# An agent attention with a gated feed-forward on one core: the planner's rule for column tiled TensorE steps, and the due times of the agents' stage

## The chip, the cores and the metric

The kernel runs on one core of one Trainium2 chip. The metric is the device time of one execution in microseconds (us), read as the median of several runs.

## The reference

For four batches of 12608 tokens of 128 values the reference computes attention through 49 agents, and puts each token through a feed-forward of width 1024. All in float32:

```python
s = 1 / sqrt(128)
agent_v = softmax(s * agents @ k.T) @ v          # per batch, 49 x 128
x = softmax(s * q @ agents.T) @ agent_v          # 12608 x 128
h = x @ w_in                                     # 1024 wide
u = h * softmax(h)
ln = (u - mean(u)) / sqrt(var(u) + 1e-6) * g_ln
out = ln @ w_out
```

The three weight arrays are in double precision and are converted on the chip.

## The kernel before, in words

**Agents' stage** (`phase_a`, one per batch). The 12608 keys of a batch go in 13 chunks of 1024 (the last has 320). M1 (`p1_mm`, L418) multiplies the agents with a chunk's keys. The two halves of a chunk land on the two halves of the 128 partitions, so that each matmul fills 64 of TensorE's 128 columns: a **column tiled** step. Then come a maximum (L423), an exponential (L444), a transpose on TensorE (TT, L451), a copy (L457) and M2 (`p2_mm`, L467), which multiplies with the values, again in two halves of 64 columns, and is added up on VectorE (L476). After chunk 13 a short chain ends the softmax and multiplies the result with `w_in`, which gives the batch's 49 x 1024 matrix, split into a high and a low part. This stage of batch 0 is the head of the kernel. That of batch b + 1 is fed in between the tiles of batch b.

**Queries' stage** (`phase_b`, one per unit). A unit is 8 tiles of 128 queries; a batch has 13 units. B0 (`b0`, L647) multiplies a unit's queries with the agents. It is column tiled too, two matmuls of 64 columns a tile. A maximum (L653), a subtraction (L659), an exponential, a sum and a reciprocal follow, then GpSimd's packing into high and low parts (B4, L676 to L680) and a transpose (B5, L687).

**Tiles** (99 a batch, 396 in all). For tile x, H (`c_h`, L730) gives 1024 columns in one of two wide PSUM tiles; VectorE takes the row maximum (MX, L734), ScalarE the exponential (L744), VectorE the product (U, L749) and ScalarE the sum of squares (SQ, L755). T (`c_t`, L762) transposes u in two halves, ScalarE copies the halves out (L777, L781), and VectorE or GpSimd makes high and low parts (L786, L790, L794). W (`c_w`, L810) is the last product, 24 matmuls for two tiles, into an accumulator's bank that a group of four tiles shares. GpSimd works out the scaling, which goes through DRAM to all partitions, and VectorE applies it (FIN, L875), which frees the bank.

**PSUM.** The two wide tiles aside, four banks serve everything: M1, M2, TT, B0, B5, T, the accumulators of W and a few small products. Each takes a bank and holds it until VectorE or ScalarE has read it.

**What sets the order.** The class `Plan` (L26) simulates the five queues when the kernel is built, and the order in which it places the steps is the order of the instructions on each engine; the last loop of the kernel pins it. Each step has an engine, a planned cost, a due time in units of tiles, the steps it depends on, and on TensorE a kind: 0 for H and W, 1 for transposes and others, 2 for the column tiled M1, M2 and B0. In `run`, for each engine, the steps that can start within `EPS` (0.01 us for TensorE) of the earliest one are the choice, and the one with the lowest due time goes first:

```python
s, o = min((z for z in opts if z[0] <= low + self.EPS[e]), key=lambda z: z[1].due)
```

A step that takes a bank can start no earlier than a bank is free in the simulation. `SWITCH[a][b]` is added to the planned cost of a step of kind b that follows kind a.

Due times of a tile's steps are x plus a constant (DH for H, DMX for the maximum, DT for T, DSQ for the squares, DF_ for FIN, and so on); DHR, DMXR and the like are added in the first 12 tiles, those ending in L in the last batch. B0 of the unit that starts with tile `first` is due at `first - BD0`, its later steps at `first` minus BD1 to BD5. In the agents' stage time runs in planned us: chunk c starts at z = 2.55 c, out of 38.15 in all (`total`, L552), and `at` (L553) spreads these over the batch: from ASTART before its first tile to AEND after its end, 99 + 2.04 + 3.67 = 104.71 tiles. M1 of a chunk (L574) is due at `at(z)`, M2 (L584) at `at(z + 1.5)`. M1 of chunk c waits for TT of chunk c - 2; M2 waits for its copy, the values and M2 of chunk c - 1. K and V chunks are loaded by SyncE, each two chunks ahead at most, since their buffers are two.

Of the kernel before, what the change touches and what calls it, by code (L numbers as in the profile page):

```python
# [25 lines left out]
class Plan:  # L26
# [3 lines left out]
           "AA": 0.0, "AG": 0.17, "GP": 0.25, "GD": 0.1, "GG": 0.1, "GA": 0.2}  # L30
    EPS = {"P": 0.01, "A": 0, "D": 0.07, "G": 2.6, "S": 0.0}

    SWITCH = ((0.0, 0.0, 0.0), (0.0, 0.0, 0.0), (0.087, 0.033, 0.033))

    def __init__(self, banks):
        self.banks = [[0.0, b] for b in banks]
# [25 lines left out]
    def run(self, idle=None):  # L62
        while True:
            best = None
            for e, ops in self.cand.items():
                if not ops:
                    continue
                free = [b[0] for b in self.banks if b[0] is not None]
                first = min(free) if free else None
                at, opts, low = self.at[e], [], None  # L70
                for o in ops:
                    s = max(at, o.ready[e])
                    if o.take:
                        if first is None:
                            continue
                        s = max(s, first)
                    opts.append((s, o))
                    low = s if low is None else min(low, s)
                if low is None:
                    continue  # L80
                s, o = min((z for z in opts if z[0] <= low + self.EPS[e]), key=lambda z: z[1].due)
                if o.shy > 0.0:
                    s, o = min((z for z in opts if z[0] <= s + o.shy), key=lambda z: z[1].due)
                if best is None or s < best[0]:
                    best = (s, e, o)
            if best is None:
                break
            s, e, o = best
# [17 lines left out]
            else:  # L106
                c = o.cost[o.eng.index(e)] if len(o.eng) > 1 else o.cost
# [18 lines left out]
def kernel(  # L126
# [15 lines left out]
    P = 128  # L142
# [4 lines left out]
    NCK = N // (CT * P)  # L147
# [7 lines left out]
    UB = 8  # L155
# [1 line left out]
    WC = 4  # L157

    BD0 = 13.69
    BD1 = 15.3  # L160
    BD2 = 9.96
    BD3 = -17.37
    BD4 = 0.17
    BD5 = 5.85
    DH = -3.24
    DMX = -8.66
    DEX = 0.61
    DU_ = -1.62
    DSQ = 20.92
    DT = -0.42  # L170
    DEV = -8.39
    DLD = 1.53
    DSP = -1.16
    DW = 3.3
    DR = 1.58
    DF_ = 5.14
    OUTD = -5.86
    OUTC = -74.58
    VA = 7
# [5 lines left out]
    SHY = -2.99  # L185
    DHR = -4.68
    DHL = -5.42
    DMXR = 10.02
    DMXL = 15.46
    DEXR = 5.1  # L190
    DEXL = -1.93
    DUR = -10.64
    DUL = -12.84
    DSQR = -10.36
    DSQL = -12.17
    DTR = -6.53
    DTL = -23.81
    DEVR = -0.65
    DEVL = 9.51
    DLDR = -16.59  # L200
    DLDL = 26.96
    DSPR = -6.09
    DSPL = 14.43
    DWR = 2.46
    DWL = -0.21
    RBL = 6.0
    ASTART = -3.67
    AEND = -2.04
    engs = (mybir.EngineType.PE, mybir.EngineType.Activation, mybir.EngineType.DVE, mybir.EngineType.Pool)
    SCALE = 1.0 / math.sqrt(C)  # L210
    INV = 1.0 / DF
# [151 lines left out]
    op = plan.op  # L363
# [9 lines left out]
    def phase_a(b, due, gate):  # L373

        head = b == 0
# [170 lines left out]
        def st(f, *x):  # L546
            return lambda *y: f(*x, *y)
# [2 lines left out]
        sz = lambda c: 0.524 if c < NCK else 0.164  # L550
        fr = lambda c: 1.0 if c < NCK else 0.5
        total = NC * 2.55 + 5.0  # L552
        at = lambda z: due[0] + (due[1] - due[0]) * z / total  # L553
        bg = op("G", begin, 0.0, at(0), gate)
        K, M1, E1, N1, V, M2, EE, TT, ET, AC = ({} for _ in range(10))

# [12 lines left out]
        for c in range(NC):  # L569
            kop(c)  # L570
            if not head:
                kop(c + 1)
            z = c * 2.55
            M1[c] = op("P", st(p1_mm, c), (0.876 if c < NCK else 0.449) + (0.8 if head and c == 0 else 0.0), at(z),  # L574
                       [K[c], M1.get(c - 1), TT.get(c - 2)], take=True, kind=2)
            E1[c] = op("D", st(p1_max, c), 0.6, at(z + 0.3), [M1[c], bg])
            N1[c] = op("D", st(p1_nm, c), 0.07, at(z + 0.4), [E1[c], N1.get(c - 1)])
            EE[c] = op("A", st(p1_exp, c), 0.665 if c < NCK else 0.742, at(z + 0.5), [N1[c], TT.get(c - 2)], free=M1[c])
            if c:
                FC[c] = op("A", st(p1_fc, c), 0.2, at(z + 0.6), [N1[c], AC.get(c - 4)])  # L580
            TT[c] = op("P", st(p2_t, c), 0.435 * fr(c), at(z + 1), [EE[c], M2.get(c - 2)], take=True)
            ET[c] = op(ETE, st(p2_et, c), (0.478 * fr(c), 0.6 * fr(c)), at(z + 1.2), [TT[c]], free=TT[c])
            vop(c)
            M2[c] = op("P", st(p2_mm, c), 1.043 if c < NCK else 0.485, at(z + 1.5),  # L584
                       [ET[c], V[c], M2.get(c - 1), AC.get(c - 2)], take=True, kind=2)
            AC[c] = op("D", st(p2_ev, c), 0.26, at(z + 1.8), [M2[c], FC.get(c), AC.get(c - 1)], free=M2[c])
        if head:
# [2 lines left out]
        z = NC * 2.55 - 1.5  # L590
# [10 lines left out]
        z = NC * 2.55 + 1.0  # L601
# [32 lines left out]
    def phase_b(k, dues, gate=()):  # L634
# [61 lines left out]
        prev, first = None, None  # L696
        for j0, j1 in chunks:
            f = (lambda px, j0=j0, j1=j1: b0(j0, j1, px)) if prev is None else (lambda j0=j0, j1=j1: b0(j0, j1))
            o = op("P", f, 0.155 * (j1 - j0), dues[0] + 0.1 * j0,
                   [BQ[k], prev, B0.get(k - 1)] + [B4.get((k - 2, q)) for q in range(2)] + list(gate), take=prev is None, kind=2, shy=shy)  # L700
            first = first or o
            prev = o
# [222 lines left out]
    def at(x, d, r, l):  # L925
        return x + d + (r * (1.0 - x / 12.0) if x < 12 else l if x >= (B - 1) * TB else 0.0)
# [4 lines left out]
    for x in range(n):  # L931
# [54 lines left out]
        if j == GT - 1:  # L986
            first, rest, turn, sent, d0, d1, d2 = c_rstd(G)
            o = None
# [72 lines left out]
```

## Time and profile before

| what | value |
|---|---|
| median of 3 runs | 1573.73 us (1573.48 to 1576.07) |
| the profiled execution | 1575.81 us, its span 1574.0 us |
| busy: TensorE, ScalarE, VectorE, GpSimd | 1550.8, 1440.1, 1376.5, 1254.5 us |
| granted TensorE clock, mean | 0.999 of full speed |
| moved by DMA | 133.65 MB |

The span runs from the first to the last instruction. Busy time of TensorE counts matmuls; they are pipelined and their ends are modelled, so that rows overlap, and the distance between two starts says more than a duration. Weight loads are rows of their own (PEld). In a timeline, equal instructions that follow each other are one row, with their count at the end. A float32 matmul shows as two records, so M1 of a full chunk is 4 records, M2 is 16 and B0 of a full unit is 32.

### The profile page before, as it was taken

The page shows a single profiled execution, that of the slowest core. Times are in us where ns is not written, and L with a number is a line of the kernel's source. Part 1 is how long each engine was busy: PE and PEld are TensorE (multiplying, and loading weights), DVE is VectorE, ACT ScalarE, POOL GpSimd, SP SyncE. Part 2 cuts the span into 40 slices and gives each one's busy share as a digit, 9 for nine tenths or more (in the row PEclk, how much of TensorE's full clock was granted, in tenths as well). Part 3 has the DMA queues.
Part 4 walks back from the last instruction along what each step waited for, and adds up shares of the span by engine and source line. Part 5 has one row for each costly group of instructions (what it writes and reads, how often), then busy time and mean ns, then how long its engine had stood idle before and what let it go on. Part 6 is the DMA issues. An engine that isn't in the chain of part 4 may idle for free.

```text
span 1574.0 us, 35069 instructions
## 1 busy us (share of the span) xinstructions
PE 1550.8 (99%) x12821; PEld 1381.7 (88%) x12821; DVE 1376.5 (87%) x2161; ACT 1440.1 (91%) x2740; POOL 1254.5 (80%) x1715
## 2 busy tenths in 40 slices
PE   8899999999999999999999999999999999999998
PEld 5588898998889899898899899898988989999998
DVE  6989898888998888889898888988888998989986
ACT  3599999999999999999999998999989999999996
POOL 2577888888788788787888878887878889988896
PEclk9999999999999999999999999999999999999999
DMA  9422323313123223222222232222111121111111
GB/s 370 150 88 81 96 81 95 95 59 103 62 82 100 82 88 105 91 81 74 88 68 88 88 102 88 88 88 87 49 63 53 47 69 55 62 55 49 45 42 40
DMA packets 57629, 133.65 MB, mean 85 GB/s; under 512 B 9840, under 2 KB 14064, under 8 KB 57456
## 3 DMA queue, kind: packets, MB, share of 16 engines
q1 hardware_dynamic: 57456, 131.41, 26.2%
q8 instruction: 101, 1.65, 0.4%
q14 instruction: 72, 0.59, 0.1%
HBM read 105.36 MB, written 26.02 MB: 83 GB/s over the span
## 4 chain that ended last, share of the span: by engine, by line
PE 89%; DVE 4%; ACT 3%; POOL 2%; issue 1%; DMA 0%; SPq 0%; DVEq 0%; ACTq 0%; POOLq 0%
PE px L810 33%; PE ph L730 22%; PE px L762 21%; PE px L647 3%; PE px L467 3%; PE px L418 3%; PE px L687 3%; PE px L451 1%; ACT e L744 1%; DVE u L749 1%; ACT sq L755 1%; DVE nm L734 1%; POOL uL L794 0%; ACT uT L781 0%; DVE mxp L423 0%
## 5 line engine op out<-in xcount | busy, mean ns | idle before, releaser
L794 POOL TENSOR_TENSOR uL<-uT,uH 128x1024 fp32r<-128x1024 f32 (+1 forms) x295 | 598.6, 2029 | 24.3
L734 DVE TENSOR_REDUCE nm<-ph 128x1 f32<-128x1024 f32 x396 | 480.3, 1219 | 55.3 <-PE ph L730 53.3
L749 DVE SCALAR_TENSOR_TENSOR u<-ph,e 128x1024 f32<-128x1024 f32 x396 | 481.0, 1219 | 54.2 <-ACT e L744 30.3
L755 ACT ACTIVATE sq<-u,su 128x1024 bf16<-128x1024 f32 x396 | 464.0, 1172 | 25.9 <-DVE u L749 22.8
L744 ACT ACTIVATE e<-ph,nm 128x1024 f32<-128x1024 f32 x396 | 446.3, 1132 | 28.4 <-DVE nm L734 25.0
L810 PE MATMUL px<-uL,wH 128*128 128x256 f32 x1584 | 467.2, 295 | 0.1
L810 PE MATMUL px<-uH,wH 128*128 128x256 f32 x1584 | 453.5, 286 | 2.6 <-DVE uL L786 1.4
L810 PE MATMUL px<-uH,wL 128*128 128x256 f32 x1584 | 449.4, 284 | 0.0
L762 PE MATMUL px<-ident,u 128*128 128x128 f32 x3168 | 429.4, 274 | 2.6 <-DVE u L749 0.7
L762 PEld LDWEIGHTS px<-ident,u 128*128 128x128 f32 x3168 | 355.6, 141 | 51.5 <-issue 18.7
L790 POOL TENSOR_SCALAR uH<-uT 128x1024 fp32r<-128x1024 f32 (+1 forms) x295 | 268.3, 909 | 85.7 <-ACT uT L781 84.6
L730 PE MATMUL ph<-mh,pT 128*128 128x512 f32 x792 | 326.3, 412 | 0.7 <-DVE u L749 0.4
L810 PEld LDWEIGHTS px<-uH,wH 128*128 128x128 f32 x1584 | 299.7, 189 | 15.4 <-issue 3.8
L730 PE MATMUL ph<-ml,pT 128*128 128x512 f32 x792 | 312.4, 394 | 0.0
L810 PEld LDWEIGHTS px<-uH,wL 128*128 128x128 f32 x1584 | 300.2, 189 | 9.6
L810 PEld LDWEIGHTS px<-uL,wH 128*128 128x128 f32 x1584 | 299.8, 189 | 9.0 <-issue 4.6
L781 ACT COPY uT<-px 128x512 f32<-128x512 f32 x492 | 272.9, 594 | 13.7 <-issue 3.0
L786 DVE TENSOR_TENSOR uL<-px,uH 128x512 fp32r<-128x512 f32 x300 | 200.9, 681 | 28.0 <-ACT uH L777 27.7
L777 ACT CAST uH<-px 128x512 fp32r<-128x512 f32 x300 | 170.1, 603 | 2.9 <-PE px L762 2.6
L730 PEld LDWEIGHTS ph<-mh,pT 128*128 128x128 f32 x792 | 149.2, 188 | 22.6 <-DVE u L749 4.6
L730 PEld LDWEIGHTS ph<-ml,pT 128*128 128x128 f32 x792 | 149.7, 189 | 17.1 <-DVE ml L543 0.2
L829 POOL TENSOR_TENSOR y<-x,nhalf 128x4 f32<-128x4 f32 x99 | 100.1, 1011 | 7.5
(119 smaller groups left out, 1469.2 us busy)
## 6 DMA issues: line engine op xcount, KB each, us to landing
rB<-dr SPq DMA_DIRECT2D x98, 256.0 KB
qt<-in_qT_dram SPq DMA_DIRECT2D x48, 512.0 KB
out_dram<-ob SPq DMA_DIRECT2D x95, 256.0 KB
kt<-in_kT_dram SPq DMA_DIRECT2D x36, 512.0 KB
vt<-in_v_dram SPq DMA_DIRECT2D x36, 512.0 KB
dr<-yr SPq DMA_DIRECT2D x392, 0.5 KB
kh<-in_kT_dram SPq DMA_DIRECT2D x12, 512.0 KB
vh<-in_v_dram SPq DMA_DIRECT2D x12, 512.0 KB
```

The lines of the kernel that those rows point to most:

```text
L730: nc.tensor.matmul(ph[:, sl], lhs, bmats[b]["mh" if m == 0 else "ml"][:, sl], start=(m == 0), stop=(m == 1))
L734: nc.vector.tensor_reduce(out=nms[x], in_=phs[x], op=ALU.max, axis=AX.X, negate=True)
L744: nc.scalar.activation(out=es[x], in_=phs[x], func=AF.Exp, bias=nms.pop(x), accum_out=st[G]["S"][:, j : j + 1])
L749: nc.vector.scalar_tensor_tensor(out=u, in0=phs[x], scalar=INV, in1=es[x], op0=ALU.mult, op1=ALU.mult, accum_out=su)
L755: nc.scalar.activation(out=sq, in_=u, func=AF.Square, bias=su, scale=-float(DF), accum_out=st[G]["Q"][:, j : j + 1])
L762: nc.tensor.transpose(pt[:, kf * P : (kf + 1) * P], us[x][0][:, k0 * P : (k0 + 1) * P], ident)
L777: nc.scalar.copy(out=uH, in_=pt)
L781: nc.scalar.copy(out=rr[x][:, hf * 4 : hf * 4 + 4, :], in_=pt)
L786: nc.vector.tensor_tensor(out=uL, in0=pt, in1=uH.bitcast(F32), op=ALU.subtract)
L790: nc.gpsimd.tensor_scalar(out=uH, in0=rr[x][:, k0:k1, :], scalar1=1.0, scalar2=0.0, op0=ALU.mult, op1=ALU.add)
L794: nc.gpsimd.tensor_tensor(out=uL, in0=rr[x][:, k0:k1, :], in1=uH.bitcast(F32), op=ALU.subtract)
L810: nc.tensor.matmul(po, wt[:, kf, :], ut[:, kf, :], start=(q == 0), stop=(q == WM - 1))
```

## The change

The planner gets a new constant, HOLD. If TensorE's last step was column tiled (`self.kind == 2`), the choice is first narrowed to column tiled steps that can start within 0.3 us of the earliest step of any kind; only if there is none does it go as before. Planned costs of entering and leaving the column tiling are changed, and those of M1, M2 and B0. The agents' stage of batches 1 to 3 is no longer spread over the batch but set to a pace: M1 of a chunk is due every 8 x 0.85 tiles, and M2 at z + 5.38 instead of z + 1.5. Many constants of due times are changed. No instruction is added or removed.

```diff
-    SWITCH = ((0.0, 0.0, 0.0), (0.0, 0.0, 0.0), (0.087, 0.033, 0.033))
+    SWITCH = ((0.0, 0.0, 0.12), (0.0, 0.0, 0.12), (0.18, 0.14, 0.0))
+
+    HOLD = 0.3
...
-                s, o = min((z for z in opts if z[0] <= low + self.EPS[e]), key=lambda z: z[1].due)
+                near = [z for z in opts if z[0] <= low + self.EPS[e]]
+                if e == "P" and self.kind == 2:
+                    near = [z for z in opts if z[0] <= low + self.HOLD and z[1].kind == 2] or near
+                s, o = min(near, key=lambda z: z[1].due)
...
-    BD1 = 15.3
-    BD2 = 9.96
-    BD3 = -17.37
-    BD4 = 0.17
+    BD1 = 13.69
+    BD2 = 4.55
+    BD3 = -15.03
+    BD4 = -7.65
-    DH = -3.24
-    DMX = -8.66
+    DH = -3.44
+    DMX = 1.93
-    DU_ = -1.62
-    DSQ = 20.92
-    DT = -0.42
+    DU_ = -2.24
+    DSQ = 25.67
+    DT = 0.29
-    DLD = 1.53
+    DLD = 0.4
-    DW = 3.3
-    DR = 1.58
-    DF_ = 5.14
+    DW = 3.29
+    DR = 2.85
+    DF_ = 10.2
-    DMXR = 10.02
+    DMXR = 7.04
-    DUR = -10.64
+    DUR = -14.51
-    DSQL = -12.17
-    DTR = -6.53
+    DSQL = -12.71
+    DTR = -16.28
-    DLDL = 26.96
+    DLDL = 27.03
-    ASTART = -3.67
-    AEND = -2.04
+    ASP = 0.85
+    MZ = 5.38
+    ASTART = -6.32
+    AEND = -4.19
...
-        at = lambda z: due[0] + (due[1] - due[0]) * z / total
+        at = lambda z: due[0] + (due[1] - due[0]) * z / total if head else due[0] + UB * ASP * z / 2.55
...
-            M1[c] = op("P", st(p1_mm, c), (0.876 if c < NCK else 0.449) + (0.8 if head and c == 0 else 0.0), at(z),
+            M1[c] = op("P", st(p1_mm, c), (0.95 if c < NCK else 0.51) + (0.8 if head and c == 0 else 0.0), at(z),
...
-            M2[c] = op("P", st(p2_mm, c), 1.043 if c < NCK else 0.485, at(z + 1.5),
+            M2[c] = op("P", st(p2_mm, c), 0.96 if c < NCK else 0.45, at(z + MZ) if not head else at(z + 1.5),
...
-            o = op("P", f, 0.155 * (j1 - j0), dues[0] + 0.1 * j0,
+            o = op("P", f, 0.128 * (j1 - j0), dues[0] + 0.1 * j0,
```

## Rows read from the trace of the kernel before

**Rows 1.** The page: busy time by engine, and the chain by engine.

```profile
PE 1550.8 (99%) x12821; PEld 1381.7 (88%) x12821; DVE 1376.5 (87%) x2161; ACT 1440.1 (91%) x2740; POOL 1254.5 (80%) x1715
...
PE 89%; DVE 4%; ACT 3%; POOL 2%; issue 1%; DMA 0%; SPq 0%; DVEq 0%; ACTq 0%; POOLq 0%
```

**Rows 2.** Windows: stretch and length, each engine's busy us (instructions), clock, DMA share, GB/s.

```profile
0.00:85.00 85.00, 70.91 (x625) 47.69 (x626) 64.65 (x130) 38.97 (x89) 32.59 (x48) 0.98 0.65 241
85.00:1180.00 1095.00, 1092.77 (x9060) 976.23 (x9059) 964.63 (x1514) 1028.37 (x1959) 885.40 (x1209) 1.00 0.28 85
1180.00:1540.00 360.00, 357.68 (x2912) 330.65 (x2912) 326.25 (x489) 353.42 (x659) 315.85 (x433) 1.00 0.16 52
```

**Rows 3.** Timeline of TensorE, a lone M2: start us, us, engine, line, operation, count.

```profile
510.81 0.28 PE L810 MATMUL px<-uH,wL 128*128 128x256 f32 x1
510.93 0.28 PE L810 MATMUL px<-uH,wH 128*128 128x256 f32 x1
511.14 1.09 PE L467 MATMUL px<-vt,eT 128*64 128x128 f32 x16
512.17 0.55 PE L762 MATMUL px<-ident,u 128*128 128x128 f32 x3
```

**Rows 4.** Timeline of TensorE, a lone B0 and a lone M1.

```profile
970.73 1.14 PE L647 MATMUL px<-ag_sb,qt 128*64 128x49 f32 x32
971.80 0.66 PE L762 MATMUL px<-ident,u 128*128 128x128 f32 x4
...
521.97 1.08 PE L418 MATMUL px<-kt,ag_sb 128*64 128x512 f32 x4
522.97 0.66 PE L762 MATMUL px<-ident,u 128*128 128x128 f32 x4
```

**Rows 5.** Timeline of TensorE, two runs of two column tiled steps.

```profile
850.39 1.08 PE L418 MATMUL px<-kt,ag_sb 128*64 128x512 f32 x4
851.30 1.04 PE L467 MATMUL px<-vt,eT 128*64 128x128 f32 x16
852.28 0.55 PE L762 MATMUL px<-ident,u 128*128 128x128 f32 x3
...
1002.05 1.14 PE L647 MATMUL px<-ag_sb,qt 128*64 128x49 f32 x32
1003.01 1.06 PE L467 MATMUL px<-vt,eT 128*64 128x128 f32 x16
1004.00 1.18 PE L762 MATMUL px<-ident,u 128*128 128x128 f32 x8
```

**Rows 6.** Groups by line, 85 to 1180 us: records | busy us, mean ns | idle before.

```profile
L467 PE MATMUL px<-vt,eT 128*64 128x128 f32 (+1 forms) x594 | 42.7, 279 | 0.0
L418 PE MATMUL px<-kt,ag_sb 128*64 128x512 f32 (+2 forms) x156 | 40.6, 593 | 0.5 <-DVE uL L786 0.5
L647 PE MATMUL px<-ag_sb,qt 128*64 128x49 f32 x1092 | 39.2, 224 | 0.0
```

**Rows 7.** Timeline of TensorE, the first and the last of the stage's 103 runs.

```profile
85.28 1.08 PE L418 MATMUL px<-kt,ag_sb 128*64 128x512 f32 x4
86.81 1.08 PE L418 MATMUL px<-kt,ag_sb 128*64 128x512 f32 x4 [0.45 <-DVE uL L786]
...
1169.21 1.14 PE L647 MATMUL px<-ag_sb,qt 128*64 128x49 f32 x32
```

**Rows 8.** List of TensorE's waits, 85 to 1180 us: total us, times, longest.

```profile
PE px L512 <- DVE lsp L502: 0.6, 2, 0.4
PE px L762 <- DVE rs L516: 0.6, 1, 0.6
PE px L418 <- DVE uL L786: 0.5, 1, 0.5
```

**Rows 9.** Timeline of VectorE and ScalarE: what reads the lone M1 of 521.97 us.

```profile
523.83 0.68 DVE L423 TENSOR_REDUCE mxp<-px 128x1 f32<-128x512 f32 x1
...
524.96 0.70 ACT L444 ACTIVATE ek<-px,nmp 128x512 f32<-128x512 f32 x1
```

## The prediction, on record before the changed kernel ran

> **What bounds the kernel now.** I read the page's shares first, then the chain, then the stages. TensorE is busy 99% of the span, ScalarE 91%, VectorE 87%, and 89% of the chain that ended last is TensorE's own work [rows 1]. The stages say where that holds [rows 2]: a head of 85 us in which TensorE is busy 70.91; from 85 to 1180 us, where the tiles of batches 0 to 2 run while the agents' stage of the next batch is fed in between, busy 1092.77 of 1095; from 1180 to 1540 us, batch 3 with no agents' stage, busy 357.68 of 360; the rest is the tail. In the middle no other engine is full (ScalarE 94%, VectorE 88%, GpSimd 81%), so there the time is the sum of what TensorE's steps cost, and a tenth of a microsecond saved on one comes off the end as long as TensorE is kept fed.
>
> Because ends of matmuls are modelled, I take prices from starts to starts. Matmuls of the third product follow each other at 0.11 to 0.12 us. Before a column tiled step (a matmul that fills only 64 of the array's 128 columns) the step to it is 0.21 us, at 510.93 to 511.14 [rows 3]: entering costs 0.09. Leaving costs too, and it shows in what a joined run saves. Alone, from its first start to the start of what follows, M2 took 1.03 us [rows 3], B0 1.07, M1 1.00 [rows 4]. Joined, M1 with M2 took 1.89, B0 with M2 1.95 [rows 5]. That is 1.00 + 1.03 - 1.89 = 0.14 and 1.07 + 1.03 - 1.95 = 0.15 less than the two alone, and one entry of 0.09 goes as well: **0.23 us for each run saved**.
>
> **How many runs there are.** From 85 to 1180 us there are 39 M1 (156 matmul records of four to a step), 39 M2 (594) and 36 B0 (1092) [rows 6], 114 steps. Going through the timeline they stand in 103 unbroken runs, the first at 85.28 and the last at 1169.21 us [rows 7]; only 11 runs hold two steps. The head has 20 more, batch 3 twelve lone B0.
>
> **The change, part by part.** *HOLD.* After a column tiled step the planner now takes any further column tiled step that can start within 0.3 us of the earliest, whatever its due time. *The new due times* bring such steps together. M1 was due every 2.55 x 104.71 / 38.15 = 7.0 tiles and M2 1.5 / 2.55 of that, 4.1 tiles, after its M1. Now M1 is due every 8 x 0.85 = 6.8 tiles and M2 5.38 / 2.55 x 6.8 = 14.3 tiles after it, which is 0.75 tile after the M1 two chunks later. M2 then stands ready for some ten tiles, so that nearly every M1 or B0 finds one. By due times alone 11 of 13 M2 of a batch join an M1 (33 runs saved), and if all 36 B0 joined something, 69 runs would go.
>
> PSUM banks set the limit: each of these steps takes one of four, and also the transposes and the accumulators of the third product need them. I followed each bank in the trace from its first write to its last read: at the starts of the 114 steps (first and last again in [rows 7]) other work held one bank in 30 cases, two in 51, three in 33. A run can then hold three, two or one steps without waiting, 1.97 in the mean. I take 114 / 1.97 = 58 runs, 45 fewer, and 45 x 0.23 = **10.4 us saved**. From below: 90 runs would remain if most joins fail for want of a bank or a ready step, 13 x 0.23 = 3.0 us. From above: one bank always belongs to an accumulator, so three steps a run at most, 38 runs, 65 x 0.23 = 15.0 us.
>
> *What joining costs.* The trace of before has 11 joined runs. Ten run on; in one, two M1 at 85.28 us, the second waited for a bank and TensorE sat idle for 0.45 us until VectorE had read it [rows 7]. The middle stage's list of waits has 1.7 us in four places, this one and 1.2 us at the ends of agents' stages (L512 and L516) [rows 8]. One in eleven at 0.45 is 45 x 0.04 = 1.8 us; none at all is the lower end; every run, 20 us, the upper. I take the rate that was seen, nearest to the case: **1.8 us back**. HOLD may also idle up to 0.3 us for a step nearly ready; that is part of the same bound.
>
> *Planned prices* (SWITCH, 0.95 for M1, 0.96 for M2, 0.128 a tile for B0) issue nothing; they shift the plan's clock. A lone M2 is now planned at 0.12 + 0.96 + 0.14 to 0.18 = 1.22 to 1.26 against 0.09 + 1.03 = 1.12 measured, a B0 at 1.28 to 1.32 against 1.16: the plan runs a tenth of a microsecond late on each. TensorE's instructions wait on semaphores, not on the plan's clock, so I cost this at nothing; what covers it is the queue of ready third-product and first-product matmuls.
>
> *The other due times.* The row maximum goes from 8.66 tiles early to 1.93 late, the output's scaling (FIN) from 5.14 to 10.2 late, the square from 20.9 to 25.7 late, packing of the agents' weights (B4) from on time to 7.65 late. Work on VectorE, ScalarE and GpSimd is only reordered, at the same sum; these engines have 12, 6 and 19% free in the middle [rows 2], and this covers it. If the cover fails, the row maximum delays the exponential and then the transposes, and a late FIN holds an accumulator's bank; that is the slower rival below. As TensorE has nearly no idle time to give back, nothing can be gained here either: zero in the middle.
>
> *Loads.* The number and size of DMAs stay. K chunks are asked for at the new pace, V chunks wait for M2 of two chunks before (SyncE waits in order for both). At 85 GB/s in the middle against 241 in the head [rows 2] the queues have room, so zero.
>
> *Head, batch 3, tail.* In the head TensorE is not the bound: matmuls wait there for transfers and for VectorE and ScalarE, and it idles 14 us. Some due times of the first 12 tiles change. I take zero, with 2.5 us either way, a sixth of that idle time. In batch 3, HOLD could pair some of the 12 B0, at 0.23 each: with four pairs, **0.9 us saved**. The tail stays.
>
> The sum: 10.4 - 1.8 + 0.9 = 9.5 us off; I round to 9, since both doubtful terms (HOLD's idling, a plan that is late) lean to the costly side. The profiled execution took 1575.81 us, 1574.0 of span and 1.8 around, so 1566.8; its time lies 2.1 above the median of the runs, 1573.73, so against that **1564.7 us**.
>
> **The rivals.**
>
> *Banks stay full (slower).* A joined run leaves two or three banks for VectorE and ScalarE to empty at once: M1 needs a maximum of 0.68 and an exponential of 0.70 us (B0 a maximum and a subtraction, M2 an addition) [rows 9], in queues that the tiles' own operations fill. A lone M1 at 521.97 was read last at 525.66 [rows 4, 9], so its bank was away 3.7 us, about a tile's time (396 tiles in 1574 us). With two such at once the transposes find no bank, and TensorE waits where the 0.45 us of [rows 7] is the row for it. If each of the 45 cost 0.45, it would be 20.3 - 10.4 = 9.9 us slower; it decides from 30 of 45 on (13.5 against 10.4, over 0.2%). At four in five the result is 16.2 - 10.4 = 5.8 us up, 1579.5. Against it: 1 of 11 so far, and the planner counts banks. The Trainium skill, TensorEngine Tiling (Array Packing), section PSUM Bottleneck, speaks for this rival: tiling speeds up TensorE but not the emptying of PSUM, so that the copies can become the bound. By that rule the gain would go whole; the trace so far agrees in one run of eleven.
>
> *The joins don't form (no change).* If three banks are held at most starts, or the accumulators' banks stay longer by the later FIN, the runs fall only to 90 or so: 3.0 - 0.5 = 2.5 us, 1571.2. For it: 33 of 114 starts had no bank to spare. Against: the other 81 had.
>
> *Fuller joining.* M1 of two chunks, both M2 and a B0 in runs of three, with 2 us from a luckier head: 15.0 + 2 - 1 = 16, 1557.7. Against it stand the same 33 starts.
>
> **How the numbers follow.** Forecast 0.68, its own range 1560 to 1570; fuller joining 0.12; no change 0.11; slower 0.09. The first two are faster by over 0.2% (3.1 us, about what a measurement of this kernel can tell from no change), 0.80 together; within 0.2% 0.11; slower by more 0.09. The range leaves out half of the fullest joining and the slower case: 1557.5 to 1574.5.
>
> **What would show it.** Right: the number of runs from 85 to 1180 us falls from 103 to between 45 and 70, most of them two steps long; M2 comes right behind the M1 of two chunks later or a B0; matmuls, loads and the other engines' busy time stay as they are; TensorE stays over 99% busy in a middle stage that is 8 to 11 us shorter, and head and batch 3 move by less than 3. Wrong: over 85 runs are left (joins don't form); or TensorE waits on transposes for VectorE or ScalarE after joined runs, by several us in the list of waits (banks); or the difference lies in the head; or a joined run saves under 0.15 us.

## The result, and the profile after

| | before | changed |
|---|---|---|
| median of 4 runs | 1574.24 us (1573.48 to 1576.07) | **1554.66 us** (1552.64 to 1555.49) |
| ratio | | 0.987, 95% interval 0.9857 to 0.9882 |
| profiled execution, its span | 1575.81, 1574.0 us | 1554.89, 1553.1 us |

The change is 19.6 us faster. The direction was forecast; the size was not: 1564.7 was named with a range from 1557.5 to 1574.5, and the result lies below it.

First the page of the changed kernel, the lines of [rows 1]. All lines of this kernel lie seven further down (M1 L425, M2 L474, B0 L654, H L737, T L769, W L817).

```profile
PE 1534.3 (99%) x12811; PEld 1378.1 (89%) x12811; DVE 1364.9 (88%) x2159; ACT 1438.7 (93%) x2742; POOL 1260.1 (81%) x1715
...
PE 86%; ACT 7%; DVE 5%; issue 1%; DMA 1%; POOL 0%; SPq 0%; DVEq 0%; ACTq 0%; POOLq 0%
```

TensorE is as full as before, with 16.5 us less to do. (Its ten records fewer are fillers of the head, 89 and now 79, which the planner puts into planned idle time, and three copies of eT went from VectorE to ScalarE, one of av_dup the other way: the sentence "No instruction is added or removed" holds for the rest.) To see where, both traces are cut at the same work: at the first matmul of W, and at the first W of tile 296, where batch 2 is nearly through. The windows of the kernel before, then of the changed one (columns as in [rows 2]):

```profile
0.00:76.80 76.80, 62.82 (x579) 40.21 (x579) 58.50 (x120) 32.30 (x77) 29.82 (x44) 1.00 0.72 266
76.80:1235.60 1158.80, 1155.77 (x9546) 1033.47 (x9546) 1020.96 (x1599) 1089.01 (x2073) 934.39 (x1277) 1.00 0.27 83
1235.60:1574.00 338.40, 332.20 (x2697) 308.04 (x2697) 296.99 (x444) 318.76 (x593) 290.29 (x395) 1.00 0.16 51
```

```profile
0.00:75.80 75.80, 64.05 (x569) 41.19 (x569) 57.30 (x123) 31.86 (x73) 31.78 (x44) 0.95 0.72 270
75.80:1218.70 1142.90, 1139.36 (x9534) 1029.59 (x9535) 1008.42 (x1589) 1085.70 (x2073) 935.67 (x1274) 1.00 0.26 84
1218.70:1553.10 334.40, 330.86 (x2711) 307.32 (x2710) 299.18 (x449) 321.12 (x599) 292.60 (x399) 1.00 0.17 52
```

The middle got 15.9 us shorter, the part after it 4.0, the head 1.0. The head is not steady to that: a second profile of the changed kernel (e15) has it 1.2 us shorter again, at a granted clock of 0.98 of full speed where the row above shows 0.95. Inside the middle the joined runs are plain to see. A run of five steps, M1, M2, B0, M1, M2, in TensorE's timeline of the changed kernel:

```profile
473.56 0.28 PE L817 MATMUL px<-uL,wH 128*128 128x256 f32 x1
473.68 0.28 PE L817 MATMUL px<-uH,wL 128*128 128x256 f32 x1
473.88 1.08 PE L425 MATMUL px<-kt,ag_sb 128*64 128x512 f32 x4
474.79 1.04 PE L474 MATMUL px<-vt,eT 128*64 128x128 f32 x16
475.67 1.09 PE L654 MATMUL px<-ag_sb,qt 128*64 128x49 f32 x32
476.58 1.04 PE L425 MATMUL px<-kt,ag_sb 128*64 128x512 f32 x4
477.46 1.06 PE L474 MATMUL px<-vt,eT 128*64 128x128 f32 x16
478.45 0.50 PE L737 MATMUL ph<-mh,pT 128*128 128x512 f32 x1
478.79 0.40 PE L737 MATMUL ph<-ml,pT 128*128 128x512 f32 x1
479.02 0.39 PE L737 MATMUL ph<-mh,pT 128*128 128x512 f32 x1
479.25 0.40 PE L737 MATMUL ph<-ml,pT 128*128 128x512 f32 x1
```

A step inside the run takes 0.88 to 0.99 us, where M1, M2 and B0 took 1.00, 1.03 and 1.07 alone [rows 3, 4]. The same rows show something that the prediction had passed over. After the run the first H starts at 478.45 and the second 0.34 later; the next two follow at 0.23. So the way out of the column tiling is paid in two places: in the time to the first start, and in that to the second. Banks come free while the run goes on. VectorE has read the bank of the first M2 by 476.25, before the fourth step starts, and ScalarE that of the first M1 by 477.28, before the fifth:

```profile
475.97 0.28 DVE L481 COPY av<-px 128x128 f32<-128x128 f32 x1
...
476.60 0.68 ACT L451 ACTIVATE ek<-px,nmp 128x512 f32<-128x512 f32 x1
```

**The account.** For every kernel TensorE's distances from start to start are added up in three parts. H, W and the transposes (T, TT, B5) each have a usual distance to the next start, 0.232, 0.118 and 0.109 us. Column tiled work is the distances that begin in such steps, and to it go the costs of switching found in them: 0.092 for the start that comes late on the way in, and for the second start on the way out 0.105 where H or W follows and 0.057 where a transpose does. What H, W and T take beyond all this is waits (sums of 0.2 either side of nothing are the rounding of the usual distances). In the middle, in us:

| | before | changed | difference |
|---|---|---|---|
| column tiled work and switching | 133.0 (105 runs) | 117.5 (38 runs) | -15.5 |
| of it waits inside runs (estimate) | 0.8 | 4.3 | +3.5 |
| waits in H, W, T | 8.5 | 11.6 | +3.1 |
| other small steps (ends of agents' stages) | 8.1 | 6.4 | -1.7 |
| H, W, T at their usual distances | 1009.2 | 1007.4 | -1.8 |

The second line is worked out as follows. Where no step waits, a joined step takes some 0.143 us less than a lone one (0.10 of it is the way out that is not paid: from the last matmul of an M1 it is 0.523 us to a transpose, H or W and 0.423 to a joined step): with the lone prices (1.010, 1.025 and 1.070 us for a full M1, M2 and B0) and this one figure 104 of the 105 runs before come out within 0.01 us, and 25 of the 38 runs of the changed kernel within 0.04. What the other runs take beyond it is waiting. In the changed kernel 16 steps inside runs start late, by 3.2 us together, and at each the wait ended with an operation of VectorE or ScalarE that reads a bank (L451, L483, L666, L793 or L882). One run of five, M1, M2, B0, M1, M2, waits twice; its fourth step starts 1.10 us after the third and its fifth 1.25 after the fourth, where 0.91 and 0.88 were seen above:

```profile
279.68 1.09 PE L654 MATMUL px<-ag_sb,qt 128*64 128x49 f32 x32
280.78 1.08 PE L425 MATMUL px<-kt,ag_sb 128*64 128x512 f32 x4
282.03 1.09 PE L474 MATMUL px<-vt,eT 128*64 128x128 f32 x16 [0.17 <-ACT ek L451]
```

The last line of the account is only work that moved across the cut: after it, +1.8. The rest after the cut: waits 4.6 to 0.2, other steps 1.9 to 0.5. With 1.0 in the head that is all of the 20.9 us of the two spans. (The two cuts differ a little from 85 and 1180 us, so 105 runs here are the prediction's 103.)

### The profile page after: what moved, and what is told of

Read it like the earlier page. It is cut to its first block, busy times and chain, and to the rows that moved or that the text cites. A ratio compares the mean times of both kernels' runs of the same rounds, so it can differ in the third digit from the quotient of the medians.

```text
span 1553.1 us, 35241 instructions
## 1 busy us (share of the span) xinstructions
PE 1534.3 (99%) x12811; PEld 1378.1 (89%) x12811; DVE 1364.9 (88%) x2159; ACT 1438.7 (93%) x2742; POOL 1260.1 (81%) x1715
## 4 chain that ended last, share of the span: by engine, by line
PE 86%; ACT 7%; DVE 5%; issue 1%; DMA 1%; POOL 0%; SPq 0%; DVEq 0%; ACTq 0%; POOLq 0%
PE px L817 32%; PE ph L737 22%; PE px L769 21%; PE px L694 2%; ACT e L751 2%; PE px L654 2%; PE px L474 2%; PE px L425 2%; ACT sq L762 2%; PE px L458 1%; ACT uT L788 1%; DVE u L756 1%; DVE nm L741 1%; DVE mxp L430 1%; ACT uH L784 1%
## 5 line engine op out<-in xcount | busy, mean ns | idle before, releaser
L741 DVE TENSOR_REDUCE nm<-ph 128x1 f32<-128x1024 f32 x396 | 475.4, 1214 | 53.2 <-PE ph L737 52.3
L762 ACT ACTIVATE sq<-u,su 128x1024 bf16<-128x1024 f32 x396 | 466.7, 1178 | 12.3 <-DVE u L756 9.5
L817 PE MATMUL px<-uH,wH 128*128 128x256 f32 x1584 | 464.3, 293 | 0.7 <-DVE uL L793 0.7
L769 PE MATMUL px<-ident,u 128*128 128x128 f32 x3168 | 460.7, 274 | 4.4 <-DVE u L756 3.0
L817 PE MATMUL px<-uL,wH 128*128 128x256 f32 x1584 | 462.9, 292 | 0.0
L751 ACT ACTIVATE e<-ph,nm 128x1024 f32<-128x1024 f32 x396 | 450.9, 1140 | 12.9 <-DVE nm L741 12.1
L817 PE MATMUL px<-uH,wL 128*128 128x256 f32 x1584 | 448.8, 283 | 0.0
L769 PEld LDWEIGHTS px<-ident,u 128*128 128x128 f32 x3168 | 366.3, 141 | 40.2 <-DVE u L756 4.1
L737 PE MATMUL ph<-mh,pT 128*128 128x512 f32 x792 | 334.2, 422 | 0.3 <-DVE u L756 0.2
L737 PE MATMUL ph<-ml,pT 128*128 128x512 f32 x792 | 313.0, 395 | 0.0
L817 PEld LDWEIGHTS px<-uL,wH 128*128 128x128 f32 x1584 | 299.5, 189 | 7.6 <-issue 2.1
L817 PEld LDWEIGHTS px<-uH,wH 128*128 128x128 f32 x1584 | 298.7, 189 | 6.9 <-issue 1.8
L817 PEld LDWEIGHTS px<-uH,wL 128*128 128x128 f32 x1584 | 299.3, 189 | 6.0
L788 ACT COPY uT<-px 128x512 f32<-128x512 f32 x492 | 287.2, 601 | 11.4 <-PE px L769 8.1
L793 DVE TENSOR_TENSOR uL<-px,uH 128x512 fp32r<-128x512 f32 x300 | 201.4, 683 | 23.0 <-ACT uH L784 22.8
L784 ACT CAST uH<-px 128x512 fp32r<-128x512 f32 x300 | 174.8, 611 | 4.5 <-PE px L769 4.3
L737 PEld LDWEIGHTS ph<-mh,pT 128*128 128x128 f32 x792 | 149.6, 189 | 27.3 <-issue 6.4
L737 PEld LDWEIGHTS ph<-ml,pT 128*128 128x128 f32 x792 | 150.1, 190 | 17.2
```

What stands on the lines that cost most here:

```text
L737: nc.tensor.matmul(ph[:, sl], lhs, bmats[b]["mh" if m == 0 else "ml"][:, sl], start=(m == 0), stop=(m == 1))
L741: nc.vector.tensor_reduce(out=nms[x], in_=phs[x], op=ALU.max, axis=AX.X, negate=True)
L751: nc.scalar.activation(out=es[x], in_=phs[x], func=AF.Exp, bias=nms.pop(x), accum_out=st[G]["S"][:, j : j + 1])
L762: nc.scalar.activation(out=sq, in_=u, func=AF.Square, bias=su, scale=-float(DF), accum_out=st[G]["Q"][:, j : j + 1])
L769: nc.tensor.transpose(pt[:, kf * P : (kf + 1) * P], us[x][0][:, k0 * P : (k0 + 1) * P], ident)
L784: nc.scalar.copy(out=uH, in_=pt)
```

## The experiments

All medians stand beside the kernel before in the same session, 1574.1 to 1574.5 us; behind each stands its ratio to that kernel with the 95% interval. Differences from the changed kernel are taken from its 1554.66 us; in the last session it had 1553.34, so they are good to 1 or 2 us. The account of all kernels is in one table behind them. "Switching" is short for its column tiled work and switching, which holds the waits inside runs.

**e1, no rule.** The changed kernel without the rule:

```diff
-                near = [z for z in opts if z[0] <= low + self.EPS[e]]
-                if e == "P" and self.kind == 2:
-                    near = [z for z in opts if z[0] <= low + self.HOLD and z[1].kind == 2] or near
-                s, o = min(near, key=lambda z: z[1].due)
+                s, o = min((z for z in opts if z[0] <= low + self.EPS[e]), key=lambda z: z[1].due)
```

> The changed kernel with the HOLD rule taken out, all its constants kept. Its order of instructions has 112 runs of column tiled steps in the middle (37 with the rule, 104 in the kernel before). Theory 'switches' (the joins carry 12 to 13 of the 21 us, at 0.19 a run; the due times the other 7 to 8, in batch 3, the tail and the head): 75 runs more at 0.19 cost 14 us over the changed kernel, so about 1568 us, and batch 3 stays as fast as in the changed kernel. Rival 'due times' (the new due times carry most, the joins little): within 4 us of the changed kernel, 1554 to 1559.

1576.05 us, ratio to before 1.0012 (1.0003 to 1.0021). The whole gain is gone, and more than theory 'switches' had said: column tiled work and switching rises by 19.2, not 14. At 0.235 a run (0.143 + 0.092) 75 runs are 17.6, the late second starts add 5.9, as 66 of the 113 runs are now followed by H or W, the dearer way out, and the 4.3 us of waits inside runs go. Batch 3 did not stay fast: 4.5 us of waits after the cut. The rival falls.

**e2, the rule alone.** The kernel before with the rule, nothing else:

```diff
+    HOLD = 0.3
...
+                near = [z for z in opts if z[0] <= low + self.EPS[e]]
+                if e == "P" and self.kind == 2:
+                    near = [z for z in opts if z[0] <= low + self.HOLD and z[1].kind == 2] or near
```

> The kernel before with the HOLD rule alone; all its constants kept. Its order has 46 runs in the middle instead of 104, and 6 instead of 11 in batch 3. Theory 'switches': 58 runs fewer at 0.19 give 11 us, 5 fewer in batch 3 one more: 1562 us, with the waits of the first product on VectorE in batch 3 still there. Rival 'due times': under 4 us faster, 1570 or more. A third possibility, that joins without the retimed agents' stage collide over PSUM banks: TensorE's list of waits in the middle grows by 5 us or more and the gain is lost.

1567.16 us (0.9956, 0.9943 to 0.9968). Switching falls by 14.8, more than expected, but waits take two thirds of it back: 5.1 more in the middle and 5.4 after. The waits are not those of joined runs alone. The list of weight load waits after the middle (lines five further down than in the kernel before) has the scaling of the last group (L867), the units' transposed weights (pT) and u:

```profile
PEld px L867 <- DVE dg L862: 3.2, 1, 3.2
PEld px L767 <- ACT pT L697: 2.0, 4, 0.7
PEld ph L735 <- DVE u L754: 1.8, 6, 0.4
```

**e3, due times alone.** The kernel before with the 18 new due times of tiles and units:

```diff
-    BD1 = 15.3
+    BD1 = 13.69
...
-    DLDL = 26.96
+    DLDL = 27.03
```

> The kernel before with the 18 changed due times of tiles and units alone (no rule, old planned costs, old timing of the agents' stage). Its order has 113 runs in the middle, nine more than before. Theory 'switches': nine runs cost 1.7 us, batch 3 and tail give back 6: about 1570 us, the gain all after 1180 us. Rival 'due times': 15 us faster or more, 1559 or less.

1582.21 us (1.0046, 1.0033 to 1.0058): slower than before. Without the rule the due times are a loss: they make 67 of 114 runs leave for H or W (19 of 105 before), 4.8 us of switching, with 3.8 more waits in the middle. Both theories missed it.

**e4, old due times.** The changed kernel with the same 18 put back, the diff of e3 the other way round:

```diff
-    BD1 = 13.69
+    BD1 = 15.3
...
-    DLDL = 27.03
+    DLDL = 26.96
```

> The changed kernel with the 18 due times of tiles and units put back (rule, planned costs and agents' timing kept). Its order has 38 runs in the middle, one more than the changed kernel, and 6 in batch 3. Theory 'switches': the middle as in the changed kernel, and 5 to 7 us lost in batch 3, tail and head: 1560 to 1562 us. Rival 'due times': 12 us or more lost, 1567 or more.

1566.10 us (0.9943, 0.993 to 0.9957). Switching is the changed kernel's, 117.5. The 11.4 us lost are waits: 7.3 more in the middle, 5.7 after. Theory 'switches' had the middle unharmed, which is wrong. Due times that are worth less than nothing alone (e3) are worth 11 us behind the rule.

**e5, runs of two.**

```diff
-                if e == "P" and self.kind == 2:
+                if e == "P" and self.kind == 2 and self.joined < 2:
...
+                    self.joined = self.joined + 1 if o.kind == 2 and self.kind == 2 else 1
```

> The changed kernel with the rule limited to runs of two steps: after two joined column tiled steps the choice goes by due time again. Its order has 63 runs in the middle (51 of two steps, 12 lone) instead of 37; this is about the count that the prediction had assumed (58). Theory 'length' (the forecast was half because runs become longer than the banks free at their start allow, and each run saved is worth 0.18 to 0.2 us): 26 runs more cost 4.7 to 5.2 us, 1559.5 us. Rival 'banks' (long runs hold banks and cost part of what they save): within 1.5 us of the changed kernel or faster, 1553 to 1556, with fewer waits of transposes.

1562.55 us (0.9922, 0.9909 to 0.9934), 7.9 slower than the changed kernel. 26 more runs cost 5.0 us of switching, which is what theory 'length' had for them; the 3 us beyond its 1559.5 are waits, 3.7 higher in the middle with the shorter runs. Rival 'banks' falls by the time, but what it names is there: inside the runs the waits go from 4.3 to 1.2 us. They come back outside, so that the two kernels wait about the same in the middle, 15.9 and 16.5 us. This kernel has about the number of runs that the prediction assumed.

**e6 to e8, due times in parts.** Three kernels, each the changed one with some due times put back: e6 BD1 to BD4, e7 DH, DMX, DU_, DSQ, DT, DLD, DW and DMXR, e8 DR and DF_.

```diff
-    BD1 = 13.69
-    BD2 = 4.55
-    BD3 = -15.03
-    BD4 = -7.65
+    BD1 = 15.3
+    BD2 = 9.96
+    BD3 = -17.37
+    BD4 = 0.17
```

```diff
...
-    DMX = 1.93
+    DMX = -8.66
...
-    DMXR = 7.04
+    DMXR = 10.02
```

```diff
-    DR = 2.85
-    DF_ = 10.2
+    DR = 1.58
+    DF_ = 5.14
```

> The changed kernel with the four due times of the queries' stage put back (BD1 to BD4). Its order has 39 runs in the middle, 6 in batch 3. The changed kernel with all 18 due times put back lost 11.5 us: 7 in waits in the middle, 3 in batch 3, where transposes waited for ScalarE's copy of the units and for FIN. Theory 'units' (the waits come from the order of the queries' stage on ScalarE and GpSimd): 7 us or more of the 11.5 are lost, 1562 or more, and transposes wait for the copy pT in batch 3. Rival 'tiles' (they come from the order of the tiles' steps): under 3 us lost.

> The changed kernel with eight due times of the tiles' steps put back (DH, DMX, DU_, DSQ, DT, DLD, DW and DMXR), those of units, of the scaling and of FIN kept. Its order has 40 runs in the middle, 11 in batch 3. Theory 'units': within 3 us of the changed kernel, 1552 to 1558. Rival 'tiles' (the row maximum ahead of the product on VectorE makes the first product and the transposes wait): 7 us or more lost, 1562 or more, with TensorE's waits for u on VectorE in batch 3 as in the kernel before.

> The changed kernel with the due times of the scaling and of FIN put back (DR 1.58, DF_ 5.14). Its order has 38 runs in the middle. The accumulators' banks come free earlier. Theory 'FIN in the way' (an early FIN stands before the product and the splits on VectorE): 3 us or more lost. Rival 'banks' (a late FIN holds a bank that the transposes want): 1 us or more gained. If neither, within 1.5 us of 1554.7.

e6 1570.74 us (0.9976, 0.9966 to 0.9986), e7 1558.98 (0.9899, 0.9885 to 0.9913), e8 1561.16 (0.9919, 0.9907 to 0.9932). The four due times of the queries' stage weigh most: 16.1 us, 6.5 of it waits in the middle and 7.5 after, while e8 loses 6.5 and e7 4.3, between its two theories. e6's weight load waits after the middle begin with the copy that theory 'units' had named, though at 2.4 us it is only a part:

```profile
PEld px L769 <- ACT pT L699: 2.4, 4, 0.9
...
PEld px L817 <- ACT uT L788: 1.5, 2, 0.8
PEld ph L737 <- DVE u L756: 1.3, 3, 0.6
```

e8's loss is 8.9 us more waits in the middle and none after, so the later scaling and FIN help there; that an early FIN stands in VectorE's way, as the theory has it, is not shown. The parts do not add up to e4's 11.4: e6 alone loses more than all 18 do. DUR, DSQL, DTR and DLDL were not put back by themselves.

**e9, leaving for a transpose.**

```diff
-                    near = [z for z in opts if z[0] <= low + self.HOLD and z[1].kind == 2] or near
+                    near = [z for z in opts if z[0] <= low + self.HOLD and z[1].kind == 2] or [z for z in opts if z[0] <= low + 0.3 and z[1].kind == 1] or near
```

> The changed kernel with one more clause: if no column tiled step is ready, TensorE leaves the column tiling for a transpose that can start within 0.3 us, if there is one. In the traces so far the second matmul of the third or first product right after a column tiled run starts 0.1 us late, and a transpose there does not. The order has 33 runs in the middle, 7 of them followed by the first or third product (37 and 30 in the changed kernel). Theory 'price': column tiled work with its switches, 117.1 us of the middle stage in the changed kernel, falls by 23 x 0.1 + 4 x 0.2 = 3.1 us to 114; with the other waits as they were 1551.5 us. Rival 'order' (the constants fit one order, and any other order brings waits of its own): the switches fall all the same, but other waits grow by 4 us or more, as in the runs before, and the time is 1555 us or more.

1552.30 us (0.9862, 0.9849 to 0.9876), between the two theories. Switching fell by 1.2 only. Four runs fewer (0.9) and cheaper second starts (1.4) are 2.3, and 1.1 more of waits inside the runs take from it. The expectation took leaving for a transpose as free, and it is not: from the first of four transposes to the fourth start it is 0.383 us behind a run and 0.327 behind W (medians of 17 and 500 groups of the changed kernel). In e16, the same kernel, four transposes behind M2 take 0.42 us to the next start, where four behind W take 0.355 (median). The account holds this price already.

```profile
473.76 1.04 PE L474 MATMUL px<-vt,eT 128*64 128x128 f32 x16
474.73 0.66 PE L769 MATMUL px<-ident,u 128*128 128x128 f32 x4
475.15 0.47 PE L737 MATMUL ph<-mh,pT 128*128 128x512 f32 x1
```

**e10 to e12.** The changed kernel with HOLD at 0.01 (e10), with the old planned costs (e11), with the old timing of the agents' stage (e12).

```diff
-    HOLD = 0.3
+    HOLD = 0.01
```

```diff
-    SWITCH = ((0.0, 0.0, 0.12), (0.0, 0.0, 0.12), (0.18, 0.14, 0.0))
+    SWITCH = ((0.0, 0.0, 0.0), (0.0, 0.0, 0.0), (0.087, 0.033, 0.033))
...
-            o = op("P", f, 0.128 * (j1 - j0), dues[0] + 0.1 * j0,
+            o = op("P", f, 0.155 * (j1 - j0), dues[0] + 0.1 * j0,
```

```diff
...
-        at = lambda z: due[0] + (due[1] - due[0]) * z / total if head else due[0] + UB * ASP * z / 2.55
+        at = lambda z: due[0] + (due[1] - due[0]) * z / total
...
```

> The changed kernel with HOLD at 0.01 us instead of 0.3: only steps that are ready at once are joined, TensorE never waits for one. 41 runs in the middle instead of 37. If the waiting of up to 0.3 us is worth something: 4 runs at 0.2 and no more, under 1 us in column tiled work and switches. Theory 'order': the time still moves by 3 us or more, in other waits. Rival (the waiting itself costs): 1 to 3 us faster than the changed kernel.

> The changed kernel with the old planned costs (SWITCH and those of M1, M2 and B0). 34 runs in the middle instead of 37. By the prediction's step these costs are worth nothing; column tiled work and switches stay within 1 us of 117. Theory 'order': the time moves by 3 us or more nonetheless, in the other waits, since the plan's clock decides which step is ready when. If the prediction's step holds: within 1.5 us of 1554.7.

> The changed kernel with the agents' stage timed as before (spread over the batch, M2 at 1.5). 50 runs in the middle instead of 37. Theory 'length': 13 runs more cost 13 x 0.17 to 0.2 = 2.2 to 2.6 us in column tiled work and switches, to 119.5. Theory 'order' adds 3 us or more of other waits: 1560 or more. Rival (the timing by units of q carries the change): 10 us or more lost, 1565 or more.

e10 1556.87 us (0.9895, 0.9881 to 0.9908): about 2 us slower, with 6.9 more waits in the middle, 1.6 less switching (four runs more, but 2.6 less of waits inside them) and a head 3.0 shorter (71.7 against 74.7 us, 73.5 in e15); waiting 0.3 us for a step is worth little by itself. e11 1554.44 (0.9874, 0.986 to 0.9887): nothing, as the prediction had it. Column tiled work did not stay within 1 us of 117: three runs fewer, but 3.4 more of waits inside them, make it 2.0 more, and the other waits are 2.6 less. Theory 'order' (any other order brings its own waits) falls here by the time. e12 1567.48 (0.9963, 0.995 to 0.9977): 12.8 lost, 2.1 in switching as theory 'length' said, 7.5 and 5.5 in waits. That is over the 10 us that the rival asked for: the timing counts, by the waits more than by the runs.

**e13 to e16, what was still open.** e13 is e2's kernel with the new BD1 to BD4; e14 is e4's with the same four, so that only 14 are put back; e15 is the changed kernel again; e16 is e9's kernel beside it.

```diff
-    BD1 = 15.3
-    BD2 = 9.96
-    BD3 = -17.37
-    BD4 = 0.17
+    BD1 = 13.69
+    BD2 = 4.55
+    BD3 = -15.03
+    BD4 = -7.65
```

> The kernel before with the rule and the four due times of the queries' stage (BD1 to BD4), nothing else. 46 runs in the middle, as with the rule alone. Theory 'units' (these four due times remove the waits after 1180 us; in all kernels with the rule that have them new and the agents' timing new, the waits there are 0.5 to 0.8 us except one with 2.2, and 6 to 10 us with them old): the waits after 1180 us fall from 10.1 us with the rule alone to 2 or less, 1559 to 1561 us. Rival 'all together' (only the full set of constants does it): 5 us of waits or more stay there, 1564 or more.

> The changed kernel with 14 of the 18 due times put back, all but BD1 to BD4. 39 runs in the middle. With all 18 put back: 19.7 us of waits in the middle and 5.9 after 1180 us. Theory 'units': 2 or less after 1180 us, and in the middle 5 or more of the 7.7 us that the old ones cost come back: 1555 to 1558 us. Rival 'all together': 1562 or more.

> The changed kernel once more, on the same chip as the next one: 1552.6 to 1555.5 us.

> The kernel that leaves the column tiling for a transpose, beside the changed kernel. Theory 'price': 2 to 3 us below it. Rival 'order': within 1 us of it or above.

e13 1559.55 us (0.9905, 0.9892 to 0.9919): the rule and four due times make 15.0 of some 20 us, with waits after the middle down from 10.0 to 2.5. e14 1563.38 (0.9937, 0.9924 to 0.9951): 7.7 of waits stay after the middle, as rival 'all together' had it, so the four due times do it in one setting and not in the other. e15 1553.34 and e16 1553.28 us, both 0.9864: leaving for transposes saves 1.2 of switching and gives 1.5 back in waits in the middle (11.3 to 12.8), as rival 'order' had it. No version beats the changed kernel.

The account, in us (spans of the profiled executions):

| kernel | span | runs in the middle (to H or W) | column tiled and switching | of it waits inside runs (estimate) | waits, middle | waits, after |
|---|---|---|---|---|---|---|
| before | 1574.0 | 105 (19) | 133.0 | 0.8 | 8.5 | 4.6 |
| changed | 1553.1 | 38 (31) | 117.5 | 4.3 | 11.6 | 0.2 |
| e1 no rule | 1573.6 | 113 (66) | 136.7 | -0.1 | 11.9 | 4.5 |
| e2 rule alone | 1565.0 | 47 (14) | 118.2 | 2.3 | 13.6 | 10.0 |
| e3 due times alone | 1578.0 | 114 (67) | 137.8 | 0.7 | 12.3 | 4.2 |
| e4 old due times | 1563.1 | 39 (25) | 117.5 | 3.5 | 18.9 | 5.9 |
| e5 runs of two | 1560.8 | 64 (43) | 122.5 | 1.2 | 15.3 | 0.0 |
| e6 old units | 1568.8 | 40 (36) | 119.1 | 5.1 | 18.1 | 7.7 |
| e7 old tiles | 1556.5 | 41 (32) | 116.5 | 2.4 | 16.5 | 1.7 |
| e8 old scaling | 1559.0 | 39 (32) | 116.9 | 3.4 | 20.5 | 0.1 |
| e10 HOLD 0.01 | 1555.0 | 42 (29) | 115.9 | 1.7 | 18.5 | -0.1 |
| e11 old costs | 1552.8 | 35 (21) | 119.5 | 7.7 | 9.0 | 0.1 |
| e12 old agents' timing | 1565.3 | 51 (43) | 119.6 | 2.1 | 19.1 | 5.7 |
| e13 rule, units | 1556.9 | 47 (16) | 118.4 | 3.3 | 12.0 | 2.5 |
| e14 units of 18 | 1560.2 | 40 (30) | 117.4 | 3.7 | 14.6 | 7.7 |
| e15 changed again | 1551.7 | 38 (31) | 117.5 | 4.4 | 11.3 | 0.4 |
| e16 leaving for T | 1550.1 | 34 (8) | 116.3 | 5.4 | 12.8 | -0.2 |

The column tiled work falls with the number of runs in the large, from 137.8 at 114 over 122.5 at 64 to 118 at 47 (e2 and e4 have one B0 more in the middle). From 34 to 42 runs it goes from 115.9 to 119.5 in no such order, and the two highest, e11 and e6, are near the top in waits inside the runs. The waits do not follow the runs at all: for 34 to 51 runs those in H, W and T go from 9.0 to 20.5 in the middle.

## Why the prediction was right or wrong

**The bound, right.** TensorE was and is 99% busy, and what its steps cost comes off the end.

**The price of a run, right for what it counted.** 0.23 us was taken for the way in and the distance to the first start behind, and 0.235 is what both are where nothing waits: 15.7 us for 67 runs. The late second starts, which it had not counted, went down by 3.2 as well (19 x 0.105 + 86 x 0.057 = 6.9 before, 31 x 0.105 + 7 x 0.057 = 3.7 now). The waits inside the runs went up by 3.5. That 15.5 us for 67 runs come to 0.23 again is luck: the last two nearly cancel.

**The number of runs: the step that failed.** "A run can then hold three, two or one steps without waiting, 1.97 in the mean" gave 58 runs and 10.4 us; 38 runs and 15.5 us came, beyond the end of 15.0 given from above. The count took the banks held at a run's start as held all through it. A step lasts 0.9 us and a lone M1's bank was away 3.7 us, so banks come free while the run goes on: there are four, and five steps went through in 4.57 us, with the bank of M2 read 1.46 us after that step's start. Where none is free yet, the run waits for one and goes on. e5, kept to runs of two, has 122.5 us of column tiled work and switching, 10.5 below the kernel before: about the forecast's 10.4, from 41 runs saved instead of 45. The end given from above was 38 runs, and that is the number that came, but it allowed no run over three steps, and runs of six stand among them.

**What joining costs, too low.** 1.8 us were given back in the forecast for waits at joined steps; inside the runs 3.5 came, at a like rate (4.3 us over 78 joins are 0.055 each, 0.04 was taken) over more joins. How much of the 3.1 us of waits in H, W and T belongs to the joins and how much to the other due times is not shown. The slower rival (banks stay full) has this much to it, at the joined steps themselves: 3.5 of some 19 us go back, and not all of it. That the transposes find no bank, as it says, is not shown. The rule of the Trainium skill that spoke for it, TensorEngine Tiling (Array Packing), section PSUM Bottleneck, that tiling speeds up TensorE but not the emptying of PSUM, agrees with the trace in those 3.5 us and does not decide the result.

**The other due times, the second failed step.** "Nothing can be gained here either" was said of the middle, and batch 3 was given 0.9 for pairs of B0 and the tail nothing. No pairs came: ten runs stand there in both kernels. But 4.4 us of waits and 1.4 of other small steps went after the cut. In the kernel before, H waited for u once in each unit of eight tiles (ten times, some 28 us apart), and this could have been read. The weight load waits after the middle, before and changed:

```profile
PEld ph L730 <- DVE u L749: 3.0, 10, 0.5
...
PEld px L762 <- ACT uT L781: 1.0, 1, 1.0
```

```profile
PEld px L769 <- DVE uL L793: 0.8, 4, 0.2
PEld px L769 <- DVE u L756: 0.7, 4, 0.2
PEld px L769 <- ACT uT L788: 0.5, 3, 0.2
```

What removes them is not one edit. The rule alone makes them worse (10.0); with the four due times of the queries' stage they are 2.5; putting those back into the changed kernel gives 7.7. But e14 and e12 keep the four and still wait 7.7 and 5.7. Which further constants are needed, and by what chain, stays open.

**Zero for the middle from due times, too good.** The waits of H, W and T in the middle rise by 3.1 with the whole change, and by another 6.5 to 8.9 where e4, e6, e8 or e12 take a part of it away. That the free shares of the other engines (12, 6 and 19%) would cover any reordering was wrong.

**Planned prices and loads, right.** e11 puts the first at nothing. Bytes moved are the same, and no load appears among the waits that changed.

**The forecast, in sum:** the runs saved 8.6 us short (19.0 against 10.4; 5.2 of it are 22 runs more, the rest mostly the late second starts), batch 3, tail and head 5.9 short (6.8 against 0.9), the small steps at the ends of agents' stages 1.7, and 0.5 lost to rounding down from 9.5 to 9; against it the waits inside runs 1.7 dearer than forecast (3.5 against 1.8) and those in H, W and T 3.1 (against zero). That is 11.9, the difference between 9 and 20.9 on the profiled executions. Two of the signs named for being right failed with it: the runs were to fall to between 45 and 70, most of two steps, and the middle to get 8 to 11 us shorter.

## What to carry to other kernels

Count a limited resource over the whole stretch in which it is wanted, not at its start: what comes free while the work runs decides how long a run can be. Price a change of mode up to the second instruction behind it, and look where the work leaves the mode. In an order planned for engines that are nearly full, a change of order has two accounts, the work it saves and the waits it makes; the first can be forecast from rows, the second moved by some 10 us in either part of these runs, and the range has to hold that. A sum that comes out right is not yet a working that is right: here a saving that was not counted and waits that were counted too low cancelled.

## What the runs showed of the hardware that was not expected

Leaving the column tiling shows in the second matmul behind it: after a run the second H comes 0.337 us after the first, where H follows H at 0.23, the second W 0.222 against 0.118, the second transpose 0.165 against 0.109 (medians of the middle, within 0.002 the same in the kernel before, changed and in e1, e5 and e16). Behind a transpose the second H is late too, at 0.314, but there the first one starts 0.08 early, 0.028 after the transpose instead of 0.109, which evens out; behind a run the first start is late as well, by 0.10. With the late start on the way in a lone step costs some 0.29 us beside its own work when a transpose follows, 0.09 + 0.14 + 0.06.
